# A list-scheduling planner is given a new clock, measured times and new deadlines (attention, cosine layer, PReLU layer, one core)

## The chip, the core and the metric

The kernel runs on one core of a Trainium2 chip. The core has a matmul engine (TensorE, PE in the profile), a vector engine (VectorE, DVE), a scalar engine with function tables (ScalarE, ACT), a general engine (GpSimd, POOL), and a queue processor that here issues every DMA (SyncE, SP). They run side by side and wait for each other by semaphores. PE writes its results into eight banks of a separate memory, PSUM; all other tiles lie in on-chip memory, SBUF. The metric is the time of one execution on the device in microseconds (us); lower is better.

## What is computed

Three layers in a row, all float32; only the third layer's result is written out.

```
# 1: Nystrom attention, q, k, v: 4 x 8 heads x 576 x 64, m = 32 landmarks
q_lm, k_lm = means of q and k over groups of 18 rows
A, Bm, C = softmax(q k_lm^T / 8), softmax(q_lm k_lm^T / 8), softmax(q_lm k^T / 8)
Z = Bm^T / (norm1(Bm) * norminf(Bm) + 1e-6)
for _ in range(6): Z = 2 * Z - Z @ Bm @ Z
x = (A @ Z @ C @ v), heads side by side      # 2304 x 512
# 2: h = x @ w_in (512 x 2048);  x = (h * cos(h)) @ w_out (2048 x 512)
# 3: h = x @ w_in2;  x = (max(h,0) + alpha * min(h,0)) @ w_out2
```

The second layer's weights, and the third's, arrive as 64-bit words (float64), and the kernel makes float32 of them with integer steps.

## The kernel before

The whole program is written as a list of operations, each with the engines that may do it, a duration for each, the tiles that it reads and writes and, for some, a time by which it should be done. A planner, `Plan.go`, then simulates the engines at build time and emits the operations in the order of that simulation. No order is written out by hand.

- Of every operation the planner takes a deadline `dl`: its target, or that of its successors less their durations, plus numbers from the table `ADJ`, by the operation's key ("t42" is all of block 42, "t:7" the seventh operation of every block, "t42:9" one of them). For each engine it goes through the operations that are ready and picks the one with the smallest start time plus `KA` times its slack. Of two engines that may do an operation, the one that ends it first gets it.
- Before, durations come from formulas (`pe`, `act`, `dve`, `pool`: a size over a rate plus a constant, scaled by `PS`, `AS`, `DS`, `GS`), a result is visible to others after a fixed 0.13 or 0.2 us (`LAT`), a buffer is free 0.15 us after its last use, and one number `dma_free` stands for the DMA engines. PE's own clock is modelled by `pe_time`: half rate after an idle stretch. Nothing in the simulation slows DVE beside POOL.
- Names of operations: "u0", "U2" and so on are the attention's head groups (`unit`: transposes on PE at L621, scores at L697, exponentials, the landmark sums at L633 on DVE or, later, on POOL at L673), "z" the 32 x 32 iteration (`z_path`, L857 on PE and L870 on DVE in turn), "c" a weight conversion (`convert`: a load at L492, then three DVE steps, L498, L500, L502; L525 stores what will be read again), "v" the product of Z C v with w_in (`vprime`: PE at L915, ACT at L920, DVE at L922), so that the second layer's first matmul takes attention's A directly.
- "t0" to "t127" are the blocks of the second layer (`tick`). One is: six matmuls at L959 into a PSUM bank of tag h (two exist), ACT L964, DVE L966, ACT's sine L968, DVE's product L969, which frees the bank, ACT's rounding L971, the rounding error by a subtraction on POOL or DVE (helper `sub`, L352), and twelve matmuls at L984 into four banks of tag acc. "e" writes the layer's output y1 to memory (L1011).
- "s", "o" load the third layer's weights and split them into a rounded part and its error (L1102 on ACT, L352), "y" loads y1 again in chunks of 512 tokens and forms sums for a seven-product scheme, 22 subtractions of 128x256 each (L352 on POOL or DVE), and "b" are the third layer's steps: products at L1269 (L1314 in the last chunk), L1292, L1333, L1336 on DVE, rounding at L1338, and the output product L1350. `st_` (L1362) stores the output.
- All float32 matmuls of layers 2 and 3 are made of three matmuls of rounded parts (hi x hi, hi x lo, lo x hi), which is why every tile has a rounding on ACT and a subtraction beside it.

## Time and profile before

| | |
|---|---|
| runs | 862.08, 866.56, 867.01 us (median 866.56) |
| the profiled execution | 862.28 us |
| its span, first to last instruction | 860.5 us |
| mean granted clock of PE, share of full speed | 0.978 |
| PE / DVE / ACT / POOL busy | 808.0 / 640.9 / 439.4 / 199.9 us |
| instructions | 16346 |

The span is what the trace shows, 1.8 us less than the execution's time. All times in the rows below are from the span's start. Busy time is the union of an engine's instructions; matmuls are pipelined and overlap. In a row of the timeline a second duration in brackets is the engine's idle time before the row, and behind the arrow stands what ended it.

### The profile page before, as it was taken

The page shows a single profiled execution, that of the slowest core. Times are in us where ns is not written, and L with a number is a line of the kernel's source. Part 1 is how long each engine was busy: PE and PEld are TensorE (multiplying, and loading weights), DVE is VectorE, ACT ScalarE, POOL GpSimd, SP SyncE. Part 2 cuts the span into 40 slices and gives each one's busy share as a digit, 9 for nine tenths or more (in the row PEclk, how much of TensorE's full clock was granted, in tenths as well). Part 3 has the DMA queues.
Part 4 walks back from the last instruction along what each step waited for, and adds up shares of the span by engine and source line. Part 5 has one row for each costly group of instructions (what it writes and reads, how often), then busy time and mean ns, then how long its engine had stood idle before and what let it go on. Part 6 is the DMA issues. An engine that isn't in the chain of part 4 may idle for free.

```text
span 860.5 us, 16346 instructions
## 1 busy us (share of the span) xinstructions
PE 808.0 (94%) x6193; PEld 716.6 (83%) x6193; DVE 640.9 (74%) x1296; ACT 439.4 (51%) x971; POOL 199.9 (23%) x208
## 2 busy tenths in 40 slices
...
GB/s 238 111 239 142 168 35 248 191 170 131 106 229 224 165 129 169 161 234 133 181 153 122 94 99 74 74 75 37 37 62 74 38 38 62 74 50 50 54 107 25
DMA packets 87903, 103.31 MB, mean 120 GB/s; under 512 B 35856, under 2 KB 62992, under 8 KB 87824
## 3 DMA queue, kind: packets, MB, share of 16 engines
...
q14 instruction: 31, 0.25, 0.1%
...
## 4 chain that ended last, share of the span: by engine, by line
PE 64%; DVE 18%; DMA 11%; ACT 3%; issue 2%; SPq 1%; POOL 1%; DVEq 0%; ACTq 0%; POOLq 0%
PE acc L1350 22%; PE acc L984 12%; PE h L1269 10%; PE x L1269 7%; DMA m<-in_moe_w_in_dram 6%; PE h L959 6%; DVE m L352 3%; DVE m L502 2%; DVE m L500 2%; DMA m<-in_moe_w_out_dram 2%; DVE m L969 2%; PE x L1314 1%; PE h L1314 1%; DVE m L966 1%; DVE m L498 1%
## 5 line engine op out<-in xcount | busy, mean ns | idle before, releaser
L984 PE MATMUL acc<-m,m 128*128 128x288 f32 x1536 | 239.2, 302 | 4.1 <-DVE m L352 2.2
L352 POOL TENSOR_TENSOR m<-m,m 128x288 fp32r<-128x288 f32 (+3 forms) x114 | 121.3, 1071 | 474.8 <-ACT m L971 225.9
L984 PEld LDWEIGHTS acc<-m,m 128*128 128x128 f32 x1536 | 214.6, 191 | 18.6 <-issue 8.7
L1350 PE MATMUL acc<-m,m 128*128 128x512 f32 x864 | 207.8, 391 | 0.4 <-DVE m L352 0.4
L352 DVE TENSOR_TENSOR m<-m,m 128x512 fp32r<-128x512 f32 (+4 forms) x286 | 172.7, 626 | 38.5 <-ACT m L1102 14.5
L1350 PEld LDWEIGHTS acc<-m,m 128*128 128x128 f32 x864 | 157.8, 188 | 30.6 <-DVE m L352 0.8
L959 PE MATMUL h<-m,m 128*128 128x288 f32 x768 | 130.4, 307 | 15.3 <-DVE m L969 12.5
L959 PEld LDWEIGHTS h<-m,m 128*128 128x128 f32 x768 | 111.4, 194 | 29.3 <-DVE m L969 19.4
L1269 PE MATMUL h<-m,m 128*128 128x256 f32 x768 | 106.7, 282 | 0.6 <-DVE m L349 0.3
L1269 PEld LDWEIGHTS h<-m,m 128*128 128x128 f32 x768 | 99.6, 189 | 3.3 <-DVE m L349 0.6
L1338 ACT ACTIVATE m<-m 128x512 fp32r<-128x512 f32 (+1 forms) x80 | 46.5, 588 | 108.8 <-DVE m L1336 106.3
L968 ACT ACTIVATE m<-m,quarter 128x288 f32<-128x288 f32 x128 | 67.5, 533 | 32.8 <-DVE m L966 31.9
L1269 PE MATMUL x<-m,m 128*128 128x256 f32 x576 | 81.3, 284 | 2.7 <-ACT m L347 2.7
L1269 PEld LDWEIGHTS x<-m,m 128*128 128x128 f32 x576 | 74.5, 189 | 5.2 <-ACT m L347 3.3
L971 ACT ACTIVATE m<-m 128x288 fp32r<-128x288 f32 x128 | 56.1, 442 | 42.9 <-DVE m L969 35.1
L1292 DVE TENSOR_TENSOR m<-h,m 128x512 f32<-128x512 f32 x32 | 22.0, 688 | 68.5 <-ACT m L347 68.0
L964 ACT ACTIVATE m<-h 128x288 int32<-128x288 f32 x128 | 52.0, 407 | 37.6 <-PE h L959 36.5
L347 ACT ACTIVATE m<-h 128x256 f32<-128x256 f32 (+4 forms) x94 | 36.8, 391 | 63.6 <-PE h L1269 55.1
L966 DVE SCALAR_TENSOR_TENSOR m<-h,m 128x288 f32<-128x288 f32 x128 | 57.3, 449 | 14.3 <-ACT m L964 14.0
L969 DVE TENSOR_TENSOR m<-m,h 128x288 f32<-128x288 f32 x128 | 56.9, 446 | 14.7 <-ACT m L968 13.9
L1102 ACT ACTIVATE m<-m 128x512 fp32r<-128x512 f32 x68 | 41.7, 628 | 39.9 <-DMA m<-wi2d 13.3
L1336 DVE SCALAR_TENSOR_TENSOR m<-m,m 128x512 f32<-128x512 f32 x64 | 47.6, 785 | 0.0
...
## 6 DMA issues: line engine op xcount, KB each, us to landing
...
```

The costliest lines, as they stand in the source:

```text
L352: ENG[e].tensor_tensor(o, a, b, op=ALU.subtract)
L959: nc.tensor.matmul(out=hp.t[:, 0:CW], lhsT=w_[:, js], rhs=x[:, cs], start=(i == 0), stop=(i == 5))
L964: op(act(CW, True), lambda e: nc.scalar.activation(k_.t, hp.t[:, 0:CW], AF.Copy, scale=INV2PI, bias=0.25), r=[hp], w=[k_], target=T + 0.8)
L966: op(dve(CW), lambda e: nc.vector.scalar_tensor_tensor(u.t, hp.t[:, 0:CW], INV2PI, k_.t, op0=ALU.mult, op1=ALU.subtract), r=[hp, k_], w=[u])
L968: op(act(CW), lambda e: nc.scalar.activation(u.t, u.t, AF.Sin, scale=2.0 * math.pi, bias=quarter), rw=[u], aset="sin")
L969: op(dve(CW), lambda e: nc.vector.tensor_tensor(hc.t, u.t, hp.t[:, 0:CW], op=ALU.mult), r=[hp, u], w=[hc], target=T + 2.6)
L971: op(act(CW), lambda e: nc.scalar.activation(gh.t, hc.t, AF.Copy), r=[hc], w=[gh, gl])
L984: nc.tensor.matmul(out=yg[o].t[:, 0:CW], lhsT=w_.t[:, sl], rhs=x.t, start=(j == ja and i == 0), stop=(j == jb and i == 2),)
L1269: nc.tensor.matmul(out=rv(k), lhsT=a_.t[:, p, c2, js], rhs=b_.t[:, q_, c2, 0:hw], start=(first and c2 == 0 and i == 0), stop=(c2 == 1 and ...
L1336: op(dve(w), lambda e, m_=m_, hv=hv: nc.vector.scalar_tensor_tensor(m_.t[:, 0:w], hv(), 0.0, m_.t[:, 0:w], op0=ALU.max, op1=ALU.add), r=hr ...
L1338: op(act(w), lambda e, m_=m_, gh=gh: nc.scalar.activation(gh.t[:, 0:w], m_.t[:, 0:w], AF.Copy), r=[m_], w=[gh, gl])
L1350: nc.tensor.matmul(out=ya[n][t].t, lhsT=gv(x_), rhs=r_.t, start=(st and k == 0), stop=(en and k == 2))
```

## The change

What an operation computes is untouched; what changes is the planner, and with it the order on every engine and the engine of some operations.

- A table `TIMES` gives each kind of operation (the head group, conversion, block, ... of a certain length, and the place in it) two measured times per engine: how long the engine is taken, and when the result is there. A star marks the two-input steps on DVE and POOL that share something (`con`). `HOP` gives the extra time from one engine's end to another's start.
- A DVE step marked so, while a marked POOL step runs, is stretched: the part beside POOL goes at 0.55 of its speed (`SLOW`, `longer`). POOL is not stretched.
- A DMA queue is modelled: 0.55 us for an issue, 1.3 us until it starts, each transfer's own time one after another, 0.8 us to land. Stores of the kinds c:5, e:3, e:6 and b are not planned to start earlier than 3.6 us (`SH`) after their data is there.
- Buffers become free per engine, not at one time. A switch between the kinds of matmul costs PE 0.09 or 0.25 us.
- Nearly all constants of `KN` that weigh the choice change, and `ADJ` is replaced: some 230 numbers between -6 and 6 before, some 1500 between -44 and 47 now.
- One dependence is added: of the y loads of later chunks the second half waits for the last w_out2 load (`gates["o"]`).

The core of the diff (the table and most of ADJ and TIMES left out):

```diff
-KN = dict(T0=46, TA=3.4, TBT=3.05, VE=4.0, U1=-1, U2=36, U3=66, UD=7, UZ=20, C2=48, CD=3.0, LA=4, SW=6.582, BL=0.9, PB=0.058, AB=0.1901, LM=126, JG=8, VG=8, AG=8, LW=4, LG=4, KA=0.004, KC=18.8859, DRY=0, PS=1.0002, AS=1.0, DS=0.9985, GS=0.9577, MS=1.0, ML=0.65, MD=0.939)
+KN = dict(
+    T0=46, TA=3.4, TBT=3.05, VE=4.0, U1=-1, U2=36, U3=66, UD=7, UZ=20, C2=48, CD=3.0, LA=4, SW=11.475977,
+    BL=0.15762989, PB=0.030929376, AB=0.047428005, LM=126, JG=8, VG=8, AG=8, LW=4, LG=4, KA=0.0038420293,
+    KC=18.909775, DRY=0, PM=0.0, SH=3.5997386, CS=0.55, PS=1.020104, AS=0.99592017, DS=1.0785098, GS=0.94303541,
+)
...
-    "U2:21": 0.67, "U3:4": 2.78, "U5": 0.25, "U5:14": -0.75, "U5:48": 1.66, "U6": 2.12, "U7:1": -3.84,
...
+    "": -1.0, ":1": -2.6, "U2:1": -2.1, "U2:15": -6.9, "U2:16": 0.1, "U2:19": -1.3, "U2:20": -4.5, "U2:23": 6.1,
...
+DMA_A, DMA_C, DMA_ISSUE = 1.3, 0.8, 0.55
+HOP = {
+    "PE": {"PE": 0.0, "ACT": 0.037, "DVE": 0.038, "POOL": 0.08}, "ACT": {"PE": 0.054, "POOL": 0.078},
+    "DVE": {"PE": 0.055, "POOL": 0.08}, "POOL": {"PE": 0.06},
+    "SP": {"PE": 0.1, "ACT": 0.025, "DVE": 0.025, "POOL": 0.025},
+}
+TIMES = """
+U50 1=S/0/.85 2=S/0/.9 3=S/0/.75 4=P/.248/.49 5=A/.401/.491,V/.477/.557 6=P/.245/.489 7=A/.398/.488,V/.466/.546
...
+t11 1=P/.796/.956 2=A/.314/.404 3=V/.37/.45 4=A/.444/.534 5=V/.368/.448 6=A/.353/.443 7=G/.837/.882,V/.377/.457*
+t11 8=P/.397/.557 9=P/.396/.557 10=P/.396/.557 11=P/.396/.556
...
+def times():
+    table = {}
+    for line in TIMES.split("\n"):
+        for x in line.split()[1:]:
+            i, _, t = x.partition("=")
+            es = {}
+            for y in t.rstrip("*").split(","):
+                n, a, b = y.split("/")
+                es[{"P": "PE", "A": "ACT", "V": "DVE", "G": "POOL", "S": "SP"}[n]] = float(a), float(b)
+
+            def of(engs, es=es, con=t.endswith("*")):
+                return ([(e, d if e == "SP" else es[e][0]) for e, d in engs], {e: es[e][1] for e, _ in engs}, con)
+            table[line.split()[0], i] = of
+    return table
 
...
-    LAT = {"PE": 0.2, "ACT": 0.13, "DVE": 0.13, "POOL": 0.13, "SP": 0.0, "": 0.0}
...
+        E5 = ("PE", "ACT", "DVE", "POOL", "SP")
...
+        table = times()
         for o in self.ops:
             o.dl += sum(ADJ.get(x, 0.0) for x in o.key)
-        ready = {e: [] for e in free}
+            o.est = dict.fromkeys(E5, 0.0)
+            c, i = o.key[0], o.key[1].rpartition(":")[2]
+            o.engs, o.lat, o.con = table.get((f"{c[:1]}{self.count[c]}", i), lambda engs: (engs, {}, False))(o.engs)
+            o.cls = c[:1] not in ("t", "b")
+        for b in self.bufs:
+            b.free_at = dict.fromkeys(E5, 0.0)
+        ready = {e: [] for e in E5}
         scale = {"PE": KN["PS"], "ACT": KN["AS"], "DVE": KN["DS"], "POOL": KN["GS"], "SP": 1.0}
         seq = {t: [] for t in self.caps}
-        dma_free, cur = 0.0, "exp"
+        dma_free, cur, cls = 0.0, "exp", None
...
+        def spread(x, data=True):
+            for e in E5:
+                t = x.end + HOP[x.eng].get(e, 0.033)
+                for b in x.bufs:
+                    b.free_at[e] = max(b.free_at[e], t)
+                for s, d in x.succ:
+                    if d:
+                        s.est[e] = max(s.est[e], t)
+
         def finish(x, work):
             nonlocal left
             left -= 1
             for b in x.bufs:
                 b.done += 1
-                b.free_at = max(b.free_at, x.end)
+            if x.eng:
+                spread(x)
             for s, data in x.succ:
                 s.need -= 1
-                if data:
-                    lat = 0.0 if x.eng == "PE" and all(e == "PE" for e, _ in s.engs) else self.LAT[x.eng]
-                    s.est = max(s.est, x.end + lat)
...
-                    sl = slots(o)
+                    sl = slots(o, e)
                     if sl is None:
                         continue
                     d = dict(o.engs)[e] * scale[e]
-                    s = max(free[e], o.est, sl)
+                    s = max(free[e], o.est[e], sl)
                     if e == "PE":
                         d = pe_time(s, d)
-                    if o.dma:
-                        s = max(s, dma_free - KN["BL"])
+                    if e == "SP":
+                        if o.key[1] in ("c:5", "e:3", "e:6") or o.key[0][:1] == "b":
+                            s = max(s, o.est[e] + KN["SH"])
+                        s = max(s, dma_free - DMA_A - KN["BL"])
                     dl = o.dl
                     if o.aset and o.aset != cur:
                         d, dl = d + 1.28, dl + KN["SW"]
                     if len(o.engs) > 1 and any(
-                        max(free[x], o.est, sl) + dx - BIAS.get(x, 0.0) < s + d - BIAS.get(e, 0.0)
-                        for x, dx in ((y, dy * scale[y]) for y, dy in o.engs) if x != e
+                        max(free[x], o.est[x], sl) + dx * scale[x] - BIAS.get(x, 0.0) < s + d - BIAS.get(e, 0.0)
+                        for x, dx in o.engs if x != e
                     ):
                         continue
                     key = s + KA * min(dl - s, KC)
+                    if e == "PE" and cls is not None and o.cls != cls:
+                        key += KN["PM"]
...
-            if e == "PE":
-                d = pe_time(s, o.engs[0][1] * scale[e], True)
-            free[e] = s + d
-            if o.aset:
-                cur = o.aset
-            if o.dma:
-                dma_free = max(s + KN["ML"], dma_free) + o.dma * KN["MS"]
-                o.end = dma_free + KN["MD"]
+            if e == "SP":
+                m = s
+                for _ in range(round(o.engs[0][1] / 0.5)):
+                    dma_free = max(m + DMA_A, dma_free) + o.lat[e]
+                    m += DMA_ISSUE
+                free[e], o.end = m, dma_free + DMA_C
+            elif e == "PE":
+                c = dict(o.engs)[e]
+                x = 0.0 if cls is None or o.cls == cls else 0.09 if o.cls else 0.25
+                cls = o.cls
+                d = pe_time(s, c, True)
+                free[e], o.end = s + d + x, s + o.lat[e] + d - c + x
             else:
-                o.end = s + d
+                m = s + (1.28 if o.aset and o.aset != cur else 0.0)
+                cur = o.aset or cur
+                free[e], o.end = m + dict(o.engs)[e], m + o.lat[e]
+
+                def longer(a, end):
+                    x, w = (end - a) / SLOW, pool_to - a
+                    return x - (end - a) if x <= w else w - w * SLOW
+
+                if e == "POOL" and o.con:
+                    pool_to = o.end
+                    if last is not None and last[0].con and last[0].end > m + 1e-9:
+                        y = longer(max(m, last[1]), last[0].end)
+                        free["DVE"] += y
+                        last[0].end += y
+                        spread(last[0])
+                elif e == "DVE" and o.con and pool_to > m + 1e-9:
+                    y = longer(m, o.end)
+                    free["DVE"] += y
+                    o.end += y
+                if e == "DVE":
+                    last = (o, m)
...
-        return max(free.values())
+        return max(o.end for o in self.ops)
...
+            after = after + gates.get("o", []) if n and c2 else after
...
-    est = g.go({"PE": 0.0, "ACT": 1.9, "DVE": 2.2, "POOL": 3.0, "SP": 1.2})
+    est = g.go({"PE": 0.0, "ACT": 1.9, "DVE": 2.2, "POOL": 3.0, "SP": 0.75})
```

Where it moves things, in the order of the two kernels (line numbers of the changed kernel are about 337 higher: L959 is L1296 there, L984 L1321, L621 L958, L352 L689, L498, L500 and L502 are L835, L837 and L839, L922 is L1259, L966 L1303, L969 L1306).

First place: DVE just ahead of the first v' (L922, L1259), at the program's start, of before. Names m_476 and m_510 are the third pair of converted weight tiles and the fourth, m_450 and m_461 error parts of A.

```order
L352 TENSOR_TENSOR m_450<-m_174,m_449 128x576
L352 TENSOR_TENSOR m_461<-m_174,m_460 128x576
L498 TENSOR_SCALAR m_476<-m_156 128x512
L500 SCALAR_TENSOR_TENSOR m_476<-m_156,m_476 128x512
L502 SCALAR_TENSOR_TENSOR m_476<-m_156,m_476 128x512
L922 TENSOR_TENSOR m_490<-x,m_490 128x512
L922 TENSOR_TENSOR m_491<-x,m_491 128x512
```

The same place now; m_296 is the second pair, m_472 the third:

```order
L837 SCALAR_TENSOR_TENSOR m_296<-m_160,m_296 128x512
L686 COPY m_460<-x 128x2x32
L839 SCALAR_TENSOR_TENSOR m_296<-m_160,m_296 128x512
L1120 STREAM_TRANSPOSE m_178<-m_178 128x576
L835 TENSOR_SCALAR m_472<-m_160 128x512
L837 SCALAR_TENSOR_TENSOR m_472<-m_160,m_472 128x512
L689 TENSOR_TENSOR m_475<-m_178,m_474 128x576
L1259 TENSOR_TENSOR m_479<-x,m_479 128x512
L1259 TENSOR_TENSOR m_480<-x,m_480 128x512
```

Before, both conversions of the third pair (twice the three steps) are done ahead of the first v'; now two steps of one of them.

Second place: PE at the blocks 10 to 12, with the next head group's transposes (L621, L958), of before; each h tile has six matmuls, of which one row stands here.

```order
L621 MATMUL x_892<-m203008_69,m80896_156 128x128 x3
L959 MATMUL h_901<-m41984_449,m25600_490 128x288
...
L959 MATMUL h_924<-m41984_449,m33792_547 128x288
...
L621 MATMUL x_931<-m203008_69,m80896_156 128x128 x3
L621 MATMUL x_936<-m203008_69,m80896_156 128x128 x3
L984 MATMUL acc_581<-m111872_572,m123136_799 128x288 x3
```

And now, where h_912 is block 11 and h_966 block 12:

```order
L1296 MATMUL h_912<-m41984_418,m25600_479 128x288
...
L958 MATMUL x_921<-m203008_69,m80896_160 128x128 x3
L958 MATMUL x_926<-m203008_69,m80896_160 128x128 x3
L1321 MATMUL acc_592<-m111872_542,m123136_792 128x288 x3
L958 MATMUL x_938<-m203008_69,m80896_160 128x128 x3
L1321 MATMUL acc_597<-m111872_542,m123136_792 128x288 x3
L1321 MATMUL acc_603<-m111872_542,m123136_792 128x288 x3
L1321 MATMUL acc_640<-m111872_542,m123136_792 128x288 x3
L1296 MATMUL h_966<-m41984_418,m33792_559 128x288
```

Block 12 stood directly behind block 11; now nine transposes and twelve matmuls of L1321 stand between them.

Third place: DVE while the first y chunk is split (about blocks 106 to 109), of before. Tiles m203008 are the chunk's rounding errors, m111872 the blocks'.

```order
L969 TENSOR_TENSOR m104960_532<-m104960_532,h_4795 128x288
L352 TENSOR_TENSOR m111872_572<-m104960_532,m111872_572 128x288
L966 SCALAR_TENSOR_TENSOR m104960_532<-h_4825,m104960_532 128x288
L352 TENSOR_TENSOR m44288_4423<-m41984_4411 128x256
L352 TENSOR_TENSOR m203008_4847<-m41984_4411,m203008_4847 128x256
L969 TENSOR_TENSOR m104960_532<-m104960_532,h_4825 128x288
L352 TENSOR_TENSOR m203008_4847<-m48896_4463,m203008_4847 128x256 x2
L352 TENSOR_TENSOR m44288_4423<-m48896_4463,m41984_4411 128x256
L352 TENSOR_TENSOR m111872_572<-m104960_532,m111872_572 128x288
```

And now:

```order
L1306 TENSOR_TENSOR m104960_526<-m104960_526,h_4780 128x288
L689 TENSOR_TENSOR m203008_4821<-m41984_4406,m203008_4821 128x256
L1306 TENSOR_TENSOR m104960_526<-m104960_526,h_4796 128x288
L689 TENSOR_TENSOR m111872_542<-m104960_526,m111872_542 128x288 x2
L689 TENSOR_TENSOR m0_834<-m2304_1037,m6912_1115 128x256
L689 TENSOR_TENSOR m44288_4418<-m48896_4469,m41984_4406 128x256
L689 TENSOR_TENSOR m0_834<-m2304_1037,m0_834 128x256
L1303 SCALAR_TENSOR_TENSOR m104960_526<-h_4863,m104960_526 128x288
L1303 SCALAR_TENSOR_TENSOR m104960_526<-h_4875,m104960_526 128x288
L689 TENSOR_TENSOR m203008_4821<-m2304_1037,m203008_4821 128x256
L1306 TENSOR_TENSOR m104960_526<-m104960_526,h_4863 128x288
```

On both sides several two-input subtractions (L352, L689) stand in a row between two products of the blocks (L969, L1306); of the 22 subtractions of 128x256 at this place POOL has 10 before and 17 now.

## Rows read from the trace of the kernel before

**Rows 1.** the page: TensorE's busy time, share of the span, instructions

```profile
PE 808.0 (94%) x6193; PEld 716.6 (83%) x6193; DVE 640.9 (74%) x1296; ACT 439.4 (51%) x971; POOL 199.9 (23%) x208
```

**Rows 2.** busy time by stage: stretch, us, each engine, clock share, DMA, GB/s

```profile
0.00:46.57 46.57, 30.17 (x353) 19.40 (x353) 32.59 (x82) 19.75 (x42) 7.83 (x15) 0.82 0.70 184
46.57:129.00 82.43, 68.75 (x627) 55.61 (x635) 67.64 (x145) 47.85 (x108) 29.46 (x33) 0.91 0.52 139
129.00:301.00 172.00, 166.57 (x1451) 149.20 (x1436) 143.87 (x318) 110.97 (x253) 51.24 (x61) 0.99 0.64 183
301.00:430.00 129.00, 121.03 (x1082) 107.84 (x1081) 106.49 (x234) 84.74 (x189) 43.86 (x46) 0.99 0.55 167
430.00:541.00 111.00, 107.30 (x727) 100.27 (x726) 99.82 (x187) 56.96 (x121) 30.53 (x19) 1.00 0.34 108
541.00:855.20 314.20, 314.18 (x1968) 284.24 (x1966) 190.53 (x333) 118.52 (x262) 37.01 (x35) 1.00 0.20 56
```

**Rows 3.** what PE waited for: us in total, times, longest us

```profile
PE h L959 <- DVE m L969: 12.5, 13, 3.3
...
PE h L959 <- DVE m L922: 2.4, 1, 2.4
PE acc L984 <- DVE m L352: 2.2, 2, 1.9
...
PE x L621 <- DMA m<-in_k_dram: 1.2, 1, 1.2
```

**Rows 4.** PE in order of time: start, us, what, [idle before, releaser]

```profile
77.92 3.25 PE L984 MATMUL acc<-m,m 128*128 128x288 f32 x12
82.19 1.07 PE L959 MATMUL h<-m,m 128*128 128x288 f32 x6 [1.03 <-DVE m L969]
83.10 1.74 PE L984 MATMUL acc<-m,m 128*128 128x288 f32 x12
...
88.20 1.07 PE L959 MATMUL h<-m,m 128*128 128x288 f32 x6 [0.74 <-DVE m L969]
91.22 1.72 PE L959 MATMUL h<-m,m 128*128 128x288 f32 x6 [1.95 <-DVE m L969]
...
425.73 1.73 PE L959 MATMUL h<-m,m 128*128 128x288 f32 x6 [3.34 <-DVE m L969]
```

**Rows 5.** DVE and POOL in order of time, 380 and 416 us

```profile
379.99 0.43 DVE L498 TENSOR_SCALAR m<-m 128x512 int32<-128x512 int32 x1 [0.64 <-DMA m<-in_moe_w_in_dram]
...
381.46 3.39 POOL L1130 TENSOR_TENSOR m<-m,m 128x512 f32<-128x512 f32 x2 [1.42 <-DVE m L500]
...
381.95 1.76 DVE L502 SCALAR_TENSOR_TENSOR m<-m,m 128x512 int32<-128x512 int32 x1
...
416.08 7.55 POOL L352 TENSOR_TENSOR m<-m,m 128x256 fp32r<-128x256 f32 x8
...
419.21 4.70 DVE L352 TENSOR_TENSOR m<-m,m 128x288 fp32r<-128x288 f32 x5
```

**Rows 6.** lines by shape: count, busy us, mean ns, idle before

```profile
L969 DVE TENSOR_TENSOR m<-m,h 128x288 f32<-128x288 f32 x128 | 56.9, 446 | 14.7 <-ACT m L968 13.9
...
L502 DVE SCALAR_TENSOR_TENSOR m<-m,m 128x512 int32<-128x512 int32 x56 | 46.0, 823 | 0.2
L500 DVE SCALAR_TENSOR_TENSOR m<-m,m 128x512 int32<-128x512 int32 x56 | 43.5, 778 | 0.4
L352 DVE TENSOR_TENSOR m<-m,m 128x288 fp32r<-128x288 f32 x73 | 39.9, 547 | 7.8 <-ACT m L971 7.2
...
L922 DVE TENSOR_TENSOR m<-x,m 128x512 fp32r<-128x512 f32 x32 | 20.8, 679 | 0.3 <-ACT m L920 0.3
...
L352 POOL TENSOR_TENSOR m<-m,m 128x288 fp32r<-128x288 f32 x55 | 48.6, 887 | 229.9 <-ACT m L971 225.9 <-PE acc L984 3.0 <-PE h L959 0.9
```

**Rows 7.** all engines in order of time, the end

```profile
854.54 1.28 ACT L347 ACTIVATE m<-acc 128x512 f32<-128x512 f32 x2 [3.29 <-PE acc L1350]
855.16 2.56 SPq L1362 DMA_DIRECT2D out_dram<-m  x4
```

99 lines of the change are left out of this document (93 added, 6 removed), and 229 rows, old and new, of the table ADJ.

## The prediction

> **What bounds the kernel now.** I read the page first, then the busy time by stage, then what TensorE (PE) waited for, and last the vector engine (DVE) and GpSimd (POOL) beside those waits. PE is busy for 808.0 of 860.5 us [rows 1]. The stage table [rows 2] shows where the other 52 us lie: 46.57 - 30.17 = 16.4 us ahead of the first block matmul, 82.43 - 68.75 = 13.7 up to 129 us, 172.00 - 166.57 = 5.4 up to 301, 129.00 - 121.03 = 8.0 up to 430, 111.00 - 107.30 = 3.7 up to 541, then nothing for 314 us, and 5.3 us behind the last matmul. So a new order of the same matmuls can win only in the first 541 us and in the last 6. The order leaves all 5543 matmul rows as they are, so PE's work stays.
>
> The same table's clock column (PEclk) is 0.82 and 0.91 in the first two stages and 0.99 or 1.00 later: PE ran part of the time at the lower of its two levels, 1.2 instead of 2.4 GHz, there and in short pieces behind later waits. What it costs is seen where the same work stands at either level: twelve matmuls of L984 took 3.25 us from 77.92, behind two waits, and 1.74 from 83.10; six of L959 took 1.72 and 1.73 us at 91.22 and 425.73, against 1.07 at 82.19 [rows 4].
>
> The list of waits [rows 3] says what PE waits for once the blocks run: 12.5 us in 13 pieces for DVE's product at L969 (an h bank comes free only behind it), 2.4 us for the first v' at L922, 2.2 us for a rounding subtraction at L352. DVE is the engine in all three. Beside the long pieces stands POOL: at 381.46 POOL holds two L1130 sums for 3.39 us, and the DVE step L502 inside them takes 1.76 us; at 416.08 POOL runs eight L352 subtractions in 7.55 us, five of DVE's take 4.70 us together, and PE then waits 3.34 us [rows 4, 5]. Over the run the same shows in the means: L922, which reads a PSUM bank and one tile, takes 679 ns at 128x512, while L500 and L502, which read two SBUF tiles of that size, take 778 and 823; the rounding subtraction of 128x288 takes 547 ns where L969, of the same size from a bank, takes 446 [rows 6]. That excess is 56 x (0.099 + 0.144) = 13.6 us and 73 x 0.101 = 7.4 us of DVE time, most of it while DVE feeds PE.
>
> **The change part by part.**
>
> *Work moved between engines.* In the order, POOL loses 41 of its instructions and DVE has 25 more: 27 subtractions of 128x288, a net 5 two-input steps of 128x512, 7 of 128x576 and 2 of 128x256 come to DVE, while 16 copies and small scalings, net, go to the scalar engine (ACT). At the undisturbed prices [rows 6] that is 27 x 0.446 + 5 x 0.679 + 7 x about 0.75 (0.679 scaled from 512 to 576 columns, an estimate) + 2 x 0.4 less 16 x about 0.3 (an estimate below the 0.446 row) = 12.0 + 3.4 + 5.3 + 0.8 - 4.8 = 17 us more for DVE. Against that POOL's busy time falls by 27 x 0.887 = 24 us and more. One fifth fewer POOL instructions, taken in proportion, gives back one fifth of the 21 us of excess, 4 us; a planner that keeps the two apart could give back most of it. So DVE's sum moves by -4 to +13 us over 541 us in which it is idle for about 90 (541.0 - 32.59 - 67.64 - 143.87 - 106.49 - 99.82 = 90.6 [rows 2]). I put no term of its own on it; what counts is where it stands.
>
> *The start, to the first block.* Before, six weight conversions (three DVE steps each) stand ahead of the first v'; now four and two steps of a fifth. That takes one L498, one L500 and two L502 from ahead of L922, 0.43 + 0.778 + 2 x 0.823 = 2.9 us [rows 5, 6], and one subtraction of 128x576 comes in, 0.75. Net -2.1 us, on the engine that releases L959 at 49.65 with a wait of 2.4 [rows 3]. On the DMA queue the k load of the third head group (L579) now stands ahead of all stores; the 1.2 us that PE waited for it [rows 3] lie ahead of the same v' and are inside that figure, since both must end. Between 0 (if ACT's own chain to the first v' is as late) and -3.5, I take **-2 us**. The third block matmul group now follows the second directly, where a v' stood between; that moves a wait ahead of PE work that has to be done anyway, and I cost it at 0 here and at its full price in the second rival.
>
> *Blocks 8 to 12.* PE waited 1.03, 0.74 and 1.95 us ahead of three of the block groups between 82 and 93 us [rows 4]. They are blocks 8, 11 and 12. Before, block 12 stands directly behind block 11; now nine transposes and twelve output matmuls of L984 stand between. Twelve of those take 1.74 us [rows 4], so the 1.95 us wait is nearly covered, the 1.03 may go or stay, and the 0.74 should stay: -1.7 to -3.7, I take **-2.5 us**.
>
> *The other waits behind DVE and POOL.* What is left of the list [rows 3] is 12.5 - 3.7 = 8.8 us for L969, and 2.2 for L352: 11.0 us. The new clock stretches a DVE step that meets POOL, the old one did not, so these collisions are seen when the order is made. But the largest piece need not go: at the loading of the first y chunk (the 3.34 us of 425.73) POOL has 17 of the 22 subtractions of 128x256 in the new order, where it had 10, and five two-input DVE steps still stand in a row there between two L969. Bounds 0 and -11.0; I take four tenths, **-4.5 us**.
>
> *The clock.* With shorter waits, pieces at 1.2 GHz go too. The four rows named above cost 1.5 + 0.65 + 0.65 us, and some others like them lie in the first 129 us; bounds 0 and -5, I take **-1.5 us**.
>
> *Small waits.* The five stages hold 13.7 + 5.4 + 8.0 + 3.7 = 30.8 us of idle time, 16 of them in pieces that no row above names. The order is remade everywhere, so these are drawn anew: 0 ± 4, I take **-1 us**, since they were made by a clock that had every matmul a little short.
>
> *The end.* Before, the last two output tiles end together: both are copied on ACT, 1.28 us from 854.54, and four stores are issued in 2.56 us from 855.16 [rows 7]. Now the first of the two ends two matmul groups earlier, and ACT and DVE copy one each. The last copy need not wait for the other, half of 1.28 us, and the last two stores wait only for it: **-0.5 us** (0 to -0.7).
>
> *Stores held back.* The planner now issues weight and y stores 3.6 us behind the end that it computes. Nothing reads them soon (the y tiles and raw buffers have others in turn), loads queued behind them on the one DMA queue start earlier, and the gain of that is already in the start's term; the cost would be a buffer that comes free late, 0 to +2 us, taken as 0.
>
> Sum: -2 - 2.5 - 4.5 - 1.5 - 1 - 0.5 = -12 us. The profiled execution took 862.28 us; 850.3 would be its new time. The runs shown have a median of 866.56, and the profiled execution lies at their low end; carried to the median, 866.56 - 12 = **854.5 us**.
>
> **A rule against it.** Where POOL and a two-input DVE step meet, the row at 381.95 shows 1.76 us for a step of 0.68 [rows 5, 6]: 1.08 us more, as if it had stood still for most of the POOL sum beside it. The planner stretches such a step to at most 0.68 / 0.55 = 1.24 us, and lets POOL run on undelayed. The Trainium skill (SBUF - State Buffer, Who interferes with whom) says that the port pair is an exclusive lock, that the second comer fully blocks, and that this holds for POOL behind DVE too. The trace agrees for DVE with the 1.76 us; no row here separates it for POOL. It would make the first rival below the result.
>
> **The rivals.** (1) *Waits only change places.* The planner's error at a collision is 1.76 - 1.24 = 0.5 us on DVE; twenty such places on the path, of the about 150 two-input DVE steps that lie beside POOL in the first 541 us, would take back 10 of the 12 us. For it: the five-step row at the y load stands as it was. Against it: the counts ahead of the first v' and of block 12 are facts of the order. Time 866.56 - 2 = 864.5. (2) *Slower: DVE becomes the bound.* From 129 us on, DVE is busy 143.87 of 172 us and 106.49 of 129, and the 27 subtractions that came from POOL stand in just these stages; with the third block group also waiting for the whole chain of the first, and none of the excess given back, 17 us more of DVE work less the 2 + 2.5 + 0.5 of the firm terms is +12: 878.5 us. It decides if DVE's work on the path grows by more than the collisions give back, that is if DVE's mean at L500 and L502 stays near 0.8 us. Against it: the subtraction on DVE, 0.45 to 0.55 us, is shorter than POOL's 0.887, so each block's own chain gets shorter. (3) *The planner is right throughout.* All named waits go and half of the small ones: -3.5 - 3.7 - 11.0 - 5 - 0.7 and some of the 16: -24, 842.5 us.
>
> **How the numbers follow.** Forecast 0.45 (848 to 861), rival 1 0.30 (859 to 869), rival 2 0.10 (870 to 882), rival 3 0.15 (838 to 848). The runs of before differ by 5 us, so 1% (8.7 us, below 857.9 or above 875.2) is about what can be told from no change. Faster by over 1%: 0.15 and most of the forecast's 0.45, 0.40, together 0.55; slower by over 1%: most of rival 2, 0.08; the rest, 0.37, is within 1%. The range 844 to 868 leaves out 0.1 below and 0.1 above.
>
> **What the new profile would show.** Right: PE idle time from 46 to 129 us near 9 instead of 13.7, and the L969 waits near 6 us instead of 12.5; L502's mean near 0.75; the last two stores starting within 0.7 us of the last matmul's end; PE without a gap from about 530 us on. Wrong: a PE wait of 3 us or more at the y load as before; a wait for L969 ahead of the third block group larger than the v' wait that it replaces; DVE busy for over 0.9 of the stages from 129 to 430 us, which would be rival 2.

## The result and the profile after

The changed kernel took 852.93 us in the median of four runs (851.35 to 853.38), the kernel before 866.25 (862.08 to 867.01, one run more than stood above): a ratio of 0.9853 with a 95% interval of 0.9819 to 0.9887. The forecast was 854.5, within 844 to 868. The profiled execution of the change took 853.21 us with a span of 850.7, near the middle of its runs; that of before lies at the low end of its own. Between the two spans there are 860.5 - 850.7 = 9.8 us, between the medians 13.3. Below, places are compared in the two traces, and kernels by their medians.

The page's row on the engines answers to [rows 1]: PE's idle time falls from 52.5 to 45.2 us and its busy time, for the same 6193 records, from 808.0 to 805.5.

```profile
PE 805.5 (95%) x6193; PEld 709.9 (83%) x6193; DVE 646.2 (76%) x1321; ACT 438.4 (52%) x983; POOL 154.6 (18%) x167
```

To see where, I cut both traces at the same points of the program and not at the same times: at the start of the first block group, of the third, of the 21st, of the 108th, of the 115th (the y chunk's load lies between the last two), and at the last matmul's end. First the stretches of before, then those of after; the columns are those of [rows 2].

```profile
46.57:57.54 10.97, 6.36 (x29) 3.06 (x29) 9.35 (x17) 4.01 (x8) 2.34 (x4) 0.81 0.87 228
57.54:134.48 76.94, 67.55 (x637) 56.66 (x638) 63.70 (x140) 48.94 (x114) 27.93 (x30) 0.94 0.47 129
134.48:405.40 270.92, 262.36 (x2352) 233.54 (x2351) 223.06 (x500) 176.16 (x389) 81.39 (x93) 0.99 0.61 177
405.40:428.70 23.30, 18.79 (x129) 18.08 (x128) 20.75 (x40) 14.12 (x38) 12.91 (x13) 0.94 0.55 178
428.70:855.20 426.50, 422.79 (x2701) 385.82 (x2700) 291.49 (x522) 175.79 (x384) 67.54 (x54) 1.00 0.23 70
```

```profile
0.00:43.28 43.28, 29.87 (x352) 19.04 (x352) 32.24 (x81) 19.65 (x42) 6.24 (x14) 0.88 0.70 180
43.28:51.75 8.47, 2.85 (x13) 2.10 (x13) 8.15 (x16) 3.51 (x8) 2.26 (x4) 0.67 0.77 252
51.75:128.67 76.92, 68.27 (x665) 55.39 (x666) 66.78 (x150) 50.37 (x116) 24.53 (x27) 0.97 0.57 142
128.67:399.40 270.73, 262.36 (x2343) 231.65 (x2341) 229.35 (x513) 173.81 (x391) 56.31 (x65) 0.99 0.64 180
399.40:422.30 22.90, 22.23 (x162) 21.32 (x161) 19.71 (x36) 16.20 (x43) 19.15 (x22) 1.00 0.48 148
422.30:846.10 423.80, 419.89 (x2666) 380.41 (x2664) 289.24 (x530) 174.88 (x385) 46.14 (x37) 1.00 0.23 70
```

Stretch less PE busy is PE's idle time, and the differences are, in order: 13.4 - 16.4 = -3.0 us ahead of the first block (before: the first of [rows 2]), 5.6 - 4.6 = +1.0 up to the third group, 8.65 - 9.39 = -0.7 up to the 21st, 8.4 - 8.6 = -0.2 over the next 270 us, 0.7 - 4.5 = -3.8 at the y chunk, +0.2 for the rest, and 4.6 - 5.3 = -0.7 behind the last matmul: together -7.3. Two places make almost all of it, the start and the y chunk. The other 2.5 us are PE's busy time: in the third stretch the granted clock goes from 0.94 to 0.97, at the y chunk from 0.94 to 1.00; in the second it falls.

What falls ahead of the first block is mainly PE's waits in the attention's head groups, in the landmark sums and in the 32 x 32 iteration; one wait in that iteration, for L1202, is new. First before, then after (L1207 was L870, L970 was L633):

```profile
PE h L857 <- DVE m L870: 4.2, 4, 1.5
PE x L636 <- DVE m L633: 2.7, 2, 1.8
...
PE h L882 <- DVE m L875: 1.3, 1, 1.3
```

```profile
PE h L1194 <- DVE m L1207: 2.6, 4, 0.9
...
PE h L958 <- DVE m L1202: 1.7, 1, 1.7
PE x L973 <- DVE m L970: 1.6, 2, 1.1
```

Of the other waits, by releaser, as [rows 3] (L1296 was L959, L1306 was L969, L1259 was L922, L689 was L352, L958 was L621):

```profile
PE h L1296 <- DVE m L1306: 11.1, 10, 4.2
...
PE h L1296 <- DVE m L1259: 3.3, 2, 1.9
...
PE acc L1321 <- DVE m L689: 2.1, 3, 1.0
```

The three waits of the forecast are nearly as large as before (11.1 for 12.5, 3.3 for 2.4, 2.1 for 2.2). They lie elsewhere, as PE's timeline shows:

```profile
45.21 2.31 PE L1296 MATMUL h<-m,m 128*128 128x288 f32 x10 [1.40 <-DVE m L1259]
51.75 1.81 PE L1296 MATMUL h<-m,m 128*128 128x288 f32 x6 [4.22 <-DVE m L1306]
...
85.05 1.07 PE L1296 MATMUL h<-m,m 128*128 128x288 f32 x6 [2.89 <-DVE m L1306]
...
413.77 1.06 PE L1296 MATMUL h<-m,m 128*128 128x288 f32 x6 [0.26 <-DVE m L1306]
```

At the third group there stood before:

```profile
55.85 1.05 PE L915 MATMUL x<-m,m 64*32 64x512 f32 x4 [1.59 <-DVE m L502]
57.54 1.81 PE L959 MATMUL h<-m,m 128*128 128x288 f32 x6 [0.64 <-DVE m L969]
```

4.22 us stand ahead of the third group now (before: 0.64, and 1.59 ahead of the v' matmuls there), 2.89 ahead of block 11 (before 0.74), and 0.26 where the y chunk cost 3.34 [rows 4]. At the y chunk blocks go two by two with 21 matmuls of L1321 between them, while POOL, after one pause, works on without another (PE's rows, then POOL's, then two of DVE's ahead of them; a row names the shape of its first step, and POOL's 16 hold four of 128x288, DVE's four three of 128x256):

```profile
404.57 1.74 PE L1296 MATMUL h<-m,m 128*128 128x288 f32 x12
406.15 2.95 PE L1321 MATMUL acc<-m,m 128*128 128x288 f32 x21
408.93 1.80 PE L1296 MATMUL h<-m,m 128*128 128x288 f32 x12
410.57 2.94 PE L1321 MATMUL acc<-m,m 128*128 128x288 f32 x21
...
403.75 0.99 POOL L689 TENSOR_TENSOR m<-m,m 128x256 fp32r<-128x256 f32 x1 [0.62 <-ACT m L1529]
405.93 14.61 POOL L689 TENSOR_TENSOR m<-m,m 128x256 fp32r<-128x256 f32 x16 [1.19 <-ACT m L1529]
...
403.70 0.45 DVE L689 TENSOR_TENSOR m<-m,m 128x288 fp32r<-128x288 f32 x1
404.35 1.71 DVE L689 TENSOR_TENSOR m<-m,m 128x288 fp32r<-128x288 f32 x4 [0.20 <-ACT m L1308]
```

The row of five subtractions on DVE is still there, as the order had shown, but the five take 0.45 + 1.71 us and not 4.70 as in [rows 5]: three of the five begin in the 1.19 us in which POOL waits for ACT's roundings.

Steps by shape, as [rows 6] (L837 was L500, L839 was L502):

```profile
L1306 DVE TENSOR_TENSOR m<-m,h 128x288 f32<-128x288 f32 x128 | 57.1, 449 | 9.0 <-ACT m L1305 6.5 <-POOL m L689 1.1
L689 DVE TENSOR_TENSOR m<-m,m 128x288 fp32r<-128x288 f32 x100 | 52.3, 528 | 10.8 <-ACT m L1308 10.2 <-PE h L1296 0.2
L837 DVE SCALAR_TENSOR_TENSOR m<-m,m 128x512 int32<-128x512 int32 x56 | 45.3, 809 | 0.5
...
L839 DVE SCALAR_TENSOR_TENSOR m<-m,m 128x512 int32<-128x512 int32 x56 | 43.0, 770 | 0.3
...
L689 POOL TENSOR_TENSOR m<-m,m 128x288 fp32r<-128x288 f32 x28 | 25.9, 926 | 127.3 <-ACT m L1308 79.1 <-DMA m<-in_moe_w_in_dram 32.8 <-PE acc L1321 11.8
```

DVE has 100 of these subtractions instead of 73 and POOL 28 instead of 55. The two conversion steps still take 809 and 770 ns (778 and 823 before): in the mean they are stretched beside POOL nearly as much as before, though only 26 of the 112 begin while a POOL step runs, where 38 did.

The end answers to [rows 7]: one copy on ACT, one on DVE, and the last stores 0.7 us sooner behind the last matmul.

```profile
844.81 0.60 ACT L684 ACTIVATE m<-acc 128x512 f32<-128x512 f32 x1 [1.94 <-PE acc L1688]
...
846.17 0.69 DVE L686 COPY m<-acc 128x512 f32<-128x512 f32 x1 [2.83 <-PE acc L1688]
```

### The profile page after: what moved, and what is told of

Read it like the earlier page. It is cut to its first block, busy times and chain, and to the rows that moved or that the text cites. A ratio compares the mean times of both kernels' runs of the same rounds, so it can differ in the third digit from the quotient of the medians.

```text
span 850.7 us, 16292 instructions
## 1 busy us (share of the span) xinstructions
PE 805.5 (95%) x6193; PEld 709.9 (83%) x6193; DVE 646.2 (76%) x1321; ACT 438.4 (52%) x983; POOL 154.6 (18%) x167
## 4 chain that ended last, share of the span: by engine, by line
PE 61%; DVE 22%; DMA 6%; ACT 5%; issue 2%; POOL 2%; SPq 1%; DVEq 0%; ACTq 0%; POOLq 0%
PE acc L1688 21%; PE acc L1321 11%; PE h L1607 9%; PE x L1607 7%; PE h L1296 6%; DVE m L689 4%; DVE m L837 3%; DMA m<-in_moe_w_in_dram 3%; DVE m L839 2%; DVE m L1306 2%; DVE m L1303 2%; DVE m L835 2%; DMA m<-in_k_dram 1%; PE h L1652 1%; PE x L1652 1%
## 5 line engine op out<-in xcount | busy, mean ns | idle before, releaser
L689 DVE TENSOR_TENSOR m<-m,m 128x512 fp32r<-128x512 f32 (+4 forms) x321 | 192.4, 623 | 66.5 <-ACT m L1676 30.0
L1321 PE MATMUL acc<-m,m 128*128 128x288 f32 x1536 | 235.3, 300 | 2.7 <-DVE m L689 2.1
L1321 PEld LDWEIGHTS acc<-m,m 128*128 128x128 f32 x1536 | 211.3, 189 | 18.8 <-issue 9.1
L1688 PE MATMUL acc<-m,m 128*128 128x512 f32 x864 | 213.4, 392 | 3.1 <-POOL m L689 1.9
L1688 PEld LDWEIGHTS acc<-m,m 128*128 128x128 f32 x864 | 155.8, 188 | 32.4 <-POOL m L689 2.4
L689 POOL TENSOR_TENSOR m<-m,m 128x288 fp32r<-128x288 f32 (+3 forms) x79 | 85.7, 1099 | 395.2 <-ACT m L1308 79.1
L1296 PE MATMUL h<-m,m 128*128 128x288 f32 x768 | 125.8, 305 | 15.0 <-DVE m L1306 11.1
L1296 PEld LDWEIGHTS h<-m,m 128*128 128x128 f32 x768 | 108.2, 191 | 30.0 <-DVE m L1306 18.5
L684 ACT ACTIVATE m<-h 128x256 f32<-128x256 f32 (+4 forms) x102 | 39.7, 390 | 93.9 <-PE h L1607 83.4
L1303 DVE SCALAR_TENSOR_TENSOR m<-h,m 128x288 f32<-128x288 f32 x128 | 57.4, 451 | 9.3 <-ACT m L1301 8.5
L1306 DVE TENSOR_TENSOR m<-m,h 128x288 f32<-128x288 f32 x128 | 57.1, 449 | 9.0 <-ACT m L1305 6.5
L1010 POOL TENSOR_TENSOR m<-m 128x512 f32<-128x512 f32 (+3 forms) x48 | 38.8, 811 | 46.6 <-ACT m L684 33.7
```

Of the source, the lines that this page charges most:

```text
L689: ENG[e].tensor_tensor(o, a, b, op=ALU.subtract)
L1296: nc.tensor.matmul(out=hp.t[:, 0:CW], lhsT=w_[:, js], rhs=x[:, cs], start=(i == 0), stop=(i == 5))
L1303: op(dve(CW), lambda e: nc.vector.scalar_tensor_tensor(u.t, hp.t[:, 0:CW], INV2PI, k_.t, op0=ALU.mult, op1=ALU.subtract), r=[hp, k_], w=[u])
L1306: op(dve(CW), lambda e: nc.vector.tensor_tensor(hc.t, u.t, hp.t[:, 0:CW], op=ALU.mult), r=[hp, u], w=[hc], target=T + 2.6)
L1321: nc.tensor.matmul(out=yg[o].t[:, 0:CW], lhsT=w_.t[:, sl], rhs=x.t, start=(j == ja and i == 0), stop=(j == jb and i == 2),)
L1688: nc.tensor.matmul(out=ya[n][t].t, lhsT=gv(x_), rhs=r_.t, start=(st and k == 0), stop=(en and k == 2))
```

## The experiments

Some kernels change a number or a formula of the planner. In the others, whose edit is a *list*, the choosing loop of `Plan.go` is replaced by a list of all 4,002 steps with their engines, in the order in which the planner of before or after had issued them, so that one part can be changed and nothing else is planned anew (the extra gate for the y loads then has no say and is left out):

```diff
...
+ORDER = "...".split()
...
-        while left:
-            best = None
-            for e, lst in ready.items():
...
+        queue = [(self.ops[int(x[:-1])], dict(P="PE", A="ACT", V="DVE", G="POOL", S="SP")[x[-1]]) for x in ORDER]
+        while left:
+            for at, (o, e) in enumerate(queue):
+                if o.need == 0 and (sl := slots(o, e)) is not None:
+                    break
...
+            queue.pop(at)
+            s = max(free[e], o.est[e], sl)
```

All kernels compute the whole reference. Ratios are to the kernel before, run beside each on the same chip (its medians there 863.9 to 865.1 us); idle and busy are PE's, in the one profiled execution of each.

| kernel | median us | ratio, 95% interval | PE idle | PE busy |
|---|---|---|---|---|
| before | | | 52.5 | 808.0 |
| the change | 852.93 | 0.9853 (0.9819 to 0.9887) | 45.2 | 805.5 |
| start_only | 859.12 | 0.9929 (0.9903 to 0.9955) | 55.9 | 804.3 |
| middle_only | 858.32 | 0.9933 (0.9911 to 0.9956) | 47.6 | 811.0 |
| late_only | 860.62 | 0.9947 (0.9924 to 0.9970) | 51.7 | 806.0 |
| no_moves | 861.03 | 0.9955 (0.9939 to 0.9970) | 53.3 | 805.4 |
| no_moves_no_ports | 869.39 | 1.0053 (1.0034 to 1.0073) | 59.6 | 808.3 |
| no_moves_no_hold | 863.43 | 0.9990 (0.9963 to 1.0018) | 54.7 | 807.1 |
| no_moves_lock | 873.88 | 1.0102 (1.0063 to 1.0142) | 56.4 | 816.6 |
| old_subs_on_dve | 869.26 | 1.0049 (1.0024 to 1.0074) | 56.3 | 811.0 |
| new_subs_on_pool | 855.12 | 0.9895 (0.9858 to 0.9931) | 46.1 | 807.4 |
| third_group | 851.44 | 0.9840 (0.9810 to 0.9870) | 45.0 | 803.4 |
| block_11 | 853.39 | 0.9859 (0.9829 to 0.9890) | 44.8 | 806.7 |
| lock_list | 873.62 | 1.0116 (1.0077 to 1.0154) | 57.8 | 814.5 |

**Where in the program the gain lies.** Three lists, each the old order with one stretch of the new: up to block 12 (about 88 us), from there to block 96 (about 370 us), and from block 96 to the end.

```diff
 # start_only
-ORDER = old
+ORDER = new[:first matmul of block 12] + (the rest, in the order of old)
 # middle_only
+ORDER = old[:block 12] + new up to block 96 + (the rest, in the order of old)
 # late_only
+ORDER = old[:block 96] + (the rest, in the order of new)
```

> The new order up to the matmuls of block 12 (about 88 us), then the old order for all that is left; the list is written into the planner, so nothing is planned anew. My reading of the two traces: up to block 12 PE has lost 2.0 us less to waits and some 1 us less to the low clock, and everything behind has the old waits (3 to 4 us at the first y chunk): 866.2 - 3 = about 863. Rival, the start's gain is given back behind the seam because the old order's next wait is then longer: 866 +- 1.5. Rival, the start sets the buffers and transfers for the whole run, so that most of the 13 us come with it: below 858.

> The old order up to block 96 (about 370 us), then the new one. My reading: the 3.3 us wait at the first y chunk goes and the end gains 0.3: idle time of PE smaller by 4.3 us, time 866.2 - 4.5 = about 862, DVE's mean at the two-input conversion steps still near 0.8 us. Rival, the wait at the y chunk depends on what stands in POOL's and the transfers' queues from before: it stays, 866 +- 1.5.

> The old order up to block 12 and from block 96 on, the new order between them, as one list. It closes the sum of the parts: the whole change gave 12 to 13 us, the start alone 5.5 and the late part alone 4.6 in the median. Theory 1 (the parts add up, and between blocks 12 and 96 there are only small waits): 2 to 3 us gained, 862 to 863 beside 865, PE idle in this stretch within 1 us of before. Rival (the middle is worth as much as the others, by the lower clock pieces that go with its waits): 860 or less. Rival (nothing): 865.

The late part's time came out as expected: 0.53% or 4.6 us, and the 3.34 us wait at the y chunk is gone though all that is queued ahead of it is of the old order, so it is not a matter of what stood there before; DVE's row of five subtractions is as short as in the change (0.44 + 1.72 us). PE's idle time in its profiled execution is only 0.8 us below that of before, not the 4.3 expected. Behind the seam it has two waits that the old order had not, 1.89 us for a v' product, which the change has as well, and 1.25 us for L1306; its busy time is 2.0 less.

The start gave 0.71%, more than expected, and not evenly: five of its ten runs took 855.8 to 857.7 us, five 860.6 to 862.0. The profiled one is the slowest of them; its wait ahead of block 11 is 4.57 us, where the whole change, with the same order up to there, had 2.89. There DVE's subtraction L689 of 128x288 took 1.51 us beside POOL's steps at L1010, and the conversion behind it 1.21. What separates the two groups of runs is open: this wait makes 1.7 of the 4 to 5 us between them, and only one execution of the kernel has a trace.

For the middle my expectation of 2 to 3 us was wrong: 0.67%, 5.6 us, the time of the first rival. That rival's reason, the clock, doesn't show: PE's idle time is 4.9 us less than before's, of which 0.9 lie ahead of the first block, where the order is the old one, and its busy time is 3.0 more. The three parts sum to 1.91% beside 1.47% for the whole; with intervals of about 0.24% on each that is no contradiction, but the gain can't be told apart finer than that each third of the order has a share of 4 to 6 us.

These kernels, cut at the same points as above, also tell how far one pair of traces can be trusted. At the y chunk four traces with the old order there (before, start_only, middle_only, and old_subs_on_dve from below) have 4.3 to 4.5 us of idle time, and five with the new (the change, late_only, and new_subs_on_pool, third_group and block_11 from below) 0.6 or 0.7: that gain is the order's. Ahead of the first block four executions of the old order have 15.5 to 16.4 us and five of the new 13.4 to 15.2, in the mean 1.7 less and not 3.0. Over the 270 us ahead of the y chunk the pair shows next to nothing (8.4 for 8.6), but start_only and late_only, which have the old order for all or most of it, have 10.4 and 11.3, and middle_only, which has the new for most of it, 6.2: the profiled execution of before was a good one there, and the pair hides part of what the middle gives.

**What the new clock does without the moved deadlines.**

```diff
 # no_moves
-            o.dl += sum(ADJ.get(x, 0.0) for x in o.key)
+            o.dl += 0.0
 # no_moves_no_ports: as no_moves, and
-    SH=3.5997386, CS=0.55,
+    SH=3.5997386, CS=1.0,
 # no_moves_no_hold: as no_moves, and
-    SH=3.5997386, CS=0.55,
+    SH=0.0, CS=0.55,
```

> The new clock without any of the 1,500 moved deadlines. Theory 1 (the clock's part and the deadlines' part are about alike; the kernel's own clock puts this order 13 us behind the whole change and 4 us ahead of the old order): 860 to 866, PE idle 5 to 10 us more than with the whole change. Rival (the new clock is all of it): 853 to 856. Rival (the deadlines are all of it): over 868.

> As no_moves, and the clock doesn't see that a DVE step is stretched beside POOL. Theory 1 (seeing the meetings is a main part of what the new clock does; its own sum puts it 15 us behind no_moves): 8 to 15 us over no_moves, with more waits of PE for DVE's products and DVE's two-input conversion steps at 0.85 us or more in the mean. Rival (the meetings are not avoided in either, their mean was the same before and after the change): within 3 us of no_moves.

> As no_moves (the new clock without moved deadlines), and weight and y stores are issued as soon as the planner thinks them ready, not 3.6 us later. The order of the transfers differs from the middle of the first stage on. Theory 1 (my prediction took the hold at 0: nobody waits for these stores soon): within 3 us of no_moves (861), PE's waits for a transfer at L958 and for DVE's conversions the same to 2 us. Rival (a store issued early stands at the head of SP's queue, waits there for its producer and holds back the loads behind it): 5 us or more over no_moves, with longer PE and DVE waits for loads. Rival (the hold keeps buffers busy too long): 3 us or more below no_moves.

The clock with its constants, and with no deadline moved at all, is 0.45% faster than the old clock with its moved deadlines (204 numbers in the kernel before); the 1,513 new ones, from -52.8 to 46.7, give another 1.0%: about a third and two thirds, neither rival. Two parts of the clock were taken out. Without the shared ports the same planner is 0.98% slower (869.39 - 861.03 = 8.4 us), and slower than before. It does not work by keeping DVE and POOL apart, though: L837 and L839 take 798 and 750 ns without that part, 791 and 789 with it, against my expectation of 850 or more, and 25 of the 112 begin beside POOL without it, 33 with it. What grows is PE's waiting, 59.6 for 53.3 us, with 5.9 us for L839 ahead of v' matmuls. That a planner which counts the stretch leaves other work between a stretched step and the matmul that needs it would explain this, but it isn't shown: the plan without the ports also puts more steps on DVE (1357 for 1330, 652.3 us busy for 646.6), and the constants `KN` stay those of the change's clock. The hold of the stores came out at 2.4 us, at the edge of what the two kernels' intervals can tell from nothing (they just overlap, and the runs without it spread from 860 to 870). The measured times, the queue and the buffers by engine were not taken out one by one.

**The work moved from POOL to DVE.** Two lists in which only the engine of 41 subtractions L689 of 128x288 differs.

```diff
 # old_subs_on_dve: the old list
-... t1:7 on POOL ... t11:7 on POOL ...
+... t1:7 on DVE ... t11:7 on DVE ...      (41 of them)
 # new_subs_on_pool: the new list
-... t1:7 on DVE ... t11:7 on DVE ...
+... t1:7 on POOL ... t11:7 on POOL ...    (the same 41)
```

> The old order as a list, but the 41 rounding subtractions of 128x288 that the new order has on DVE and the old one on POOL run on DVE, each at its old place in the list. Theory 1 (the engine alone is worth little: 41 x 0.45 = 18 us more DVE work, against fewer meetings with POOL and chains that are 0.4 us shorter): within 4 us of the old kernel, DVE busy 8 to 18 us more, POOL 36 us less. Rival (moving subtractions off POOL is where the gain comes from): 858 or less. Rival (DVE becomes the bound): over 872.

> The reverse: the new order as a list, with the same 41 subtractions back on POOL. Theory 1 (the places count, and DVE has room, so an engine that is slower at each and disturbs DVE gives waits back): 3 to 9 us over the new kernel, PE's waits for L1306 and L689 4 to 8 us more. Rival (POOL is idle enough that it makes no difference): within 2 us of the new kernel. Rival (all of the gain was this move): about 866.

Moved to DVE in the old order, they cost 0.49% (4.2 us, at the edge of what I had expected); moved back to POOL in the new order they cost 0.42 points of the ratio (2.2 us by the medians), and there the intervals still touch. So the move is no gain of its own: in the old order it is a loss, and in the new one it may be worth 2 to 4 us of the 12 to 13, or nothing. DVE's busy time rose by only 8 us in the first (649.1 for 640.9), and it was not the bound. In the second I expected 4 to 8 us more of PE's waits; PE's idle time is 0.9 us more, and its busy time 1.9.

**Two waits of the new order taken away.** Both are lists of the new order with a few of DVE's conversion steps put behind a block's own steps.

```diff
 # third_group, DVE (c10, c11, c9: conversion steps; t0:3 is L1303, t0:5 L1306 of the first block)
-c10:2 c10:3 c11:2 c10:4 c11:3 t0:3 c11:4 c9:2 c9:3 t0:5 c9:4
+c10:2 t0:3 c10:3 c11:2 c10:4 t0:5 c11:3 c11:4 c9:2 c9:3 c9:4
 # block_11, DVE (c13: conversion steps; t9:3, t9:5: L1303, L1306 of block 9)
-c13:2 t7:7 c13:3 t9:3 c13:4 t9:5
+c13:2 t7:7 t9:3 c13:3 t9:5 c13:4
```

> The new order as a list, but the first block's two DVE steps (L1303, L1306) stand ahead of four and three of the weight conversion steps that stood ahead of them. Theory 1 (the 4.2 us wait ahead of the third block group is DVE's queue and nothing else): that wait falls to 1.5 to 2 us, and the time by 2 us or more against the new kernel. Rival (the conversions that now come later hold back raw buffers and the loads behind them): the wait falls too, and idle time of PE up to block 16 is the same or more, time within 1 us of the new kernel or above.

> The new order as a list, but block 9's L1303 and L1306 each stand ahead of the conversion step L837 and L839 of 128x512 that stood ahead of them beside POOL's three L1010 steps. Theory 1 (the 2.9 us wait ahead of block 11 is these two steps, stretched from 0.68 to 1.3 us beside POOL): the wait falls to about 1 us and the time by 1 to 2 us against the new kernel. Rival (waits change places): the next wait of the same stretch grows, idle time up to block 16 as before, time within 0.5 us.

In third_group the wait fell from 4.22 to 1.92 us, as expected, and 1.52 us (0.30 in the change) then stood ahead of the sixth group; ahead of block 11, where the order is the same, the wait is 1.71 instead of 2.89:

```profile
49.46 1.81 PE L1296 MATMUL h<-m,m 128*128 128x288 f32 x6 [1.92 <-DVE m L1306]
...
62.75 1.06 PE L1296 MATMUL h<-m,m 128*128 128x288 f32 x6 [1.52 <-DVE m L1306]
...
83.96 1.08 PE L1296 MATMUL h<-m,m 128*128 128x288 f32 x6 [1.71 <-DVE m L1306]
```

In block_11 the wait ahead of block 11 fell from 2.89 to 0.70, so it was these two steps. PE's idle time from the first block to the 21st group is 14.3 us in the change, 12.4 in third_group and 12.7 in block_11: most of each wait that was taken away stayed away up to there, which speaks against the reason of both rivals, though block_11's time is as its rival said. But ahead of the first block, where all three have the same order, the two executions have 1.5 and 0.5 us more idle time than the change's, and over the whole run PE's idle time is 45.0 and 44.8 us beside 45.2: what such a place gives is hardly more than one execution differs from the next. Neither time can be told from the change's (0.9840 and 0.9859 beside 0.9853). third_group has the lowest median of all, 851.44, and is in its interval no better than the change.

**How DVE and POOL share.** The rows of DVE and POOL ahead of block 11, first in the change, then in block_11:

```profile
81.60 0.81 POOL L689 TENSOR_TENSOR m<-m,m 128x288 fp32r<-128x288 f32 x1 [3.71 <-ACT m L1308]
82.37 3.38 POOL L1010 TENSOR_TENSOR m<-m 128x512 f32<-128x512 f32 x3
...
81.67 1.29 DVE L837 SCALAR_TENSOR_TENSOR m<-m,m 128x512 int32<-128x512 int32 x1
82.88 0.45 DVE L1303 SCALAR_TENSOR_TENSOR m<-h,m 128x288 f32<-128x288 f32 x1
83.25 1.38 DVE L839 SCALAR_TENSOR_TENSOR m<-m,m 128x512 int32<-128x512 int32 x1
```

```profile
77.34 0.80 POOL L689 TENSOR_TENSOR m<-m,m 128x288 fp32r<-128x288 f32 x1
82.74 1.28 POOL L689 TENSOR_TENSOR m<-m,m 128x288 fp32r<-128x288 f32 x1 [4.60 <-ACT m L1308]
...
82.69 0.68 DVE L837 SCALAR_TENSOR_TENSOR m<-m,m 128x512 int32<-128x512 int32 x1
...
84.00 1.07 PE L1296 MATMUL h<-m,m 128*128 128x288 f32 x6 [0.70 <-DVE m L1306]
```

In the change POOL's subtraction runs from 81.60 to 82.41, DVE's L837 begins at 81.67 and takes 1.29 us: the 0.74 that POOL still needs, and 0.55. In block_11 DVE's L837 is first, at 82.69; it takes its undisturbed 0.68, and POOL's subtraction behind it, 0.80 alone, takes 1.28. Over the whole trace of the change it is the same: 26 of the L837 and L839 steps begin while POOL runs a two-input step, and each lasts the rest of that step and 0.55 us (mean of 0.58 + 0.555, correlation 0.999; up to 0.65 for the three that meet only its last 0.12 us); 78 undisturbed ones take 0.685, and the eight that POOL joins later 0.63 to 0.69. Twelve of POOL's 128x288 subtractions begin inside a DVE step with two SBUF inputs; eleven last the rest of that and 0.66 or 0.67, and one, which meets its last 0.05 us, 0.80 in all. The later one is held up until the earlier has ended, on either side. That is what the Trainium skill (SBUF — State Buffer, Who interferes with whom) says of the port pair, in both directions; the traces here show both. What the later one then takes is 0.13 us less than alone. The change books it otherwise (DVE 1/0.55 as long beside POOL, POOL undisturbed), so I booked it as seen:

```diff
 # no_moves_lock: as no_moves, and in Plan.go
-                    pool_to = o.end
-                    if last is not None and last[0].con and last[0].end > m + 1e-9:
-                        y = longer(max(m, last[1]), last[0].end)
-                        free["DVE"] += y
-                        last[0].end += y
-                        spread(last[0])
-                elif e == "DVE" and o.con and pool_to > m + 1e-9:
-                    y = longer(m, o.end)
+                    if last is not None and last[0].con and free["DVE"] > m:
+                        y = free["DVE"] - m
+                        free["POOL"] += y
+                        o.end += y
+                    pool_to = free["POOL"]
+                elif e == "DVE" and o.con and pool_to > m:
+                    y = max(0.0, pool_to - m - 0.13)
 # lock_list: the new list, with steps moved where that clock got shorter
-PE 1329, DVE 1315, ACT 946, POOL 109, SP 303 steps
+of these at most 1189, 1058, 785, 82 and 215 in their old order; 55 steps on another engine
```

The second edit is larger than the "some hundred steps" of its expectation: some 670 of the 4,002 left their order or engine.

> As no_moves (the new clock without moved deadlines), but a DVE step with two SBUF inputs that meets a POOL step is booked as waiting for the POOL step's end, and a POOL step that meets such a DVE step as waiting for DVE's end; before, DVE's part beside POOL was booked as 1/0.55 as long, and POOL as undisturbed. In the traces DVE's 128x512 conversion steps that begin beside POOL last the rest of the POOL step and 0.55 us. Theory 1 (that is how the two share, and a planner that books it so finds a better order): 3 to 10 us under no_moves, 851 to 858, with POOL's and DVE's meetings fewer. Rival (the error of the old formula is small beside what the greedy choice does anyway): within 3 us of no_moves (861). Rival (booked as the change books it the order is right, and this one is worse, as that clock sums it): 870.

> The new order as a list in which some hundred steps ahead of 535 us were moved by a few places or to another engine, each move kept if a planner's clock with the waiting of no_moves_lock got shorter by it. By that clock it is 30 us better than the new order, by the clock of the change 20 us worse. Theory 1 (waiting is how DVE and POOL share): faster than the new kernel, 835 to 850. Rival (the clock of the change is nearer to the chip): 860 to 866. Rival (such moves fit the clock and not the chip, whichever it is): within 3 us of the new kernel.

Both were clearly slower, by 1.47% against no_moves and by 2.6% against the change: my theory that the truer price of a meeting makes the better order fell. lock_list did get rid of meetings: 13 of its 112 conversion steps begin beside POOL, and the steps take 714 and 748 ns in the mean. It is slower all the same. Where the time went can be seen. no_moves_lock has 3.1 us more idle time than no_moves, and PE is busy 11.2 us longer with the same matmuls, at a lower clock (0.969 to 0.972 in its four runs, 0.976 to 0.985 in the ten of no_moves); two stretches of no_moves, then of no_moves_lock:

```profile
47.00:135.00 88.00, 71.92 (x640) 54.89 (x637) 74.28 (x168) 48.36 (x107) 25.13 (x28) 0.92 0.54 143
135.00:300.00 165.00, 161.79 (x1415) 144.48 (x1416) 137.71 (x316) 109.23 (x241) 39.15 (x48) 1.00 0.69 189
```

```profile
47.00:135.00 88.00, 71.45 (x608) 55.98 (x608) 69.01 (x153) 49.28 (x103) 29.62 (x34) 0.87 0.52 137
135.00:300.00 165.00, 158.41 (x1359) 140.68 (x1358) 134.53 (x310) 104.21 (x227) 31.86 (x38) 0.98 0.62 173
```

The clock column (PEclk, the sixth figure) has 0.87 for 0.92 and 0.98 for 1.00. Why an order from that clock breaks PE's work up more is open. Three possible reasons that no run separates: the constants `KN` stay those of the change's clock; the edit books POOL's wait in full, 0.14 us more than the traces have; and the planner's table has POOL's times as they were measured, 0.84 us for its 128x288 subtraction, which takes 0.93 us in the mean of the change's trace and 0.80 undisturbed, so a clock that adds the waiting to such times counts part of it twice.

## Why the prediction came out

The time, the range and the sign were right, in part by luck. Of the six terms of the sum, three came out near their size, one of them by errors that cancel and one for a reason that the text had not seen; one was too small and two failed in the pair of traces.

- *The start, -2 us: right in size, by luck.* Its reason, fewer conversions ahead of the first v', gave 1.0 (the wait there is 1.40 for 2.38). The third group, which now follows the second directly, gives 2.0 back (4.22 for 0.64 and 1.59). The text had costed that at 0 here and kept its price for the second rival, and the sign of being wrong that it named, a wait there larger than the one it replaces, came. What made up for it are 3.0 us less ahead of the first block, in the attention's head groups, for which the sum had nothing but the 1.2 us of the k load; over nine traces they are 1.7. start_only gave 5.5 us in the median. third_group shows that 2.3 of the 4.22 are DVE's queue of conversion steps.
- *Blocks 8 to 12, -2.5 us: failed.* The order does put work ahead of block 12, but the wait moved to block 11, 2.89 for 0.74; idle time between the third and the 21st group fell by 0.7 us. The step that failed is the count from the order alone: what stands between two blocks says nothing of how long DVE's steps ahead of them take, and there two conversion steps met POOL and took 1.29 and 1.38 us. That was the warning in the rule against the change, and block_11 shows that it was these two.
- *Other waits behind DVE and POOL, -4.5 us: right in size, in the place where I did not look for it.* The text doubted the y chunk, since POOL has 17 of its 22 subtractions and five DVE steps stand in a row. 3.8 us came from just there, and -0.2 from the 270 us ahead of it. In the stretch POOL is busy 19.15 of 22.9 us, but three of the five steps begin in its pause, and the row takes 2.2 us instead of 4.70; besides, DVE has 5 of the 22 subtractions where it had 12, and 21 matmuls of L1321 stand between pairs of blocks. That the order there does it is shown (late_only, and the nine traces); which of the three it is, no run separates. The sign of being right for these waits, L1306 near 6 us, did not come: 11.1.
- *The clock, -1.5 us: too small.* PE's busy time fell by 2.5. The granted clock says the same beyond the pair: 0.975 in the mean of 64 runs of before beside the experiments, 0.981 to 0.986 in four of the change. Over all kernels the busy time went from 803.4 to 816.6, nearly as much as the idle time did (44.8 to 59.6).
- *Small waits, -1: not in this pair* (-0.2 and +0.2 in the long stretches); by the other traces the middle has fewer. *The end, -0.5: right*, 0.7. *Stores held back, 0:* 2.4 us for the hold, at the edge of what the measurement tells from 0.
- *DVE's work, between -4 and +13 us, no term:* DVE's busy time rose by 5.3 us (646.2 for 640.9), and L837 and L839 gave next to nothing back (0.809 and 0.770 for 0.778 and 0.823 us), where I expected 0.75 us for L502.

In the profiles the sum is -7.3 - 2.5 = -9.8, of -12 forecast; by the medians it is -13.3, since the execution of before that was profiled lies low among its runs. So the match of 852.9 with 854.5 is better than the terms were. PE's idle time from the first block to the 21st group, which was to be near 9 us where 13.7 had stood, is 14.3. The first rival's mechanism, waits that change places, was at work at the third group and in blocks 8 to 12, at 2 us each and not at 10. The second did not come: DVE is busy for over 0.9 of one short stretch only, 8.15 of 8.47 us at the start, and there with weight conversions. The lock of the ports holds, and did not take the gain back.
